# A branch prefetch hint on the tensor engine for the block that holds the general path

## The chip, the cores and the metric

The kernel runs on one core of a Trainium2 chip. The metric is device time in microseconds (us) of one execution, the median of three runs. Besides these runs there is one execution that the hardware profiler took; all rows below come from it. The engines are TensorE (PE: matrix products, with the weight load PEld beside it), VectorE (DVE), ScalarE (ACT), GpSimd (POOL) and SyncE (SP, which issues most transfers). Each engine runs its own stream of instructions; a q behind an engine's name means its sequencer, which reads that stream, branches, loads registers and waits on semaphores.

## The reference: three layers over 1536 tokens

```python
# linear attention with decay, 2 x 8 heads, 768 steps, head width 64
state = gamma * state + k_t v_t^T ;  y_t = scale * q_t state
# mixture of experts: 8 experts, 512 -> 1024 -> 512, one expert for a token
expert = argmax(x @ w_gate);  gate_w = softmax(x @ w_gate)[expert]
# an expert takes its first `capacity` (384) tokens, later ones give zeros
out = gate_w * (relu(x @ w1[expert]) @ w2[expert])
# feed-forward 512 -> 2048 -> 512 over all tokens
h = x @ w_in;  return (h * sigmoid(h)) @ w_out
```

## The kernel before

One function writes the whole program, in program order for each engine (a manual schedule). There are three stages.

The attention stage takes twelve blocks of 128 tokens. For each block it makes the scores, the head outputs and the state, then the gate: the expert of each token, its place among that expert's tokens (`place`) and one-hot rows from which the table of tokens for each expert is built. At its end `cnt` holds the number of tokens of each expert and `peak` the largest of them. The rows of expert 0 are transposed and split in two parts, `xthi` and `xtlo`, by `split_x` (line 555): ACT writes the high part in two casts, one for each 128 tokens, DVE the low part. The token table `tab_ps` of the other experts is made by twelve small matmuls (line 602).

Then comes the branch. An expert has `capm` = 216 slots here. The register `over` is loaded from `peak` on all five engines (line 670), and under `tc.If(over > capm)` (line 674) stands the general path: a loop over the experts that computes the tokens beyond 216. For the inputs that are timed no expert has more than 216 tokens, so each engine jumps over that block. On PE the general path is some 600 instructions of the compiled program.

Then follows the expert stage. For each of 8 experts `stage_a` (line 845, four times 24 matmuls, lines 854, 855 and 858, the product with w1) and `stage_b` (line 867, four times 24, lines 841 to 843, the product with w2). The weights come in 64 units of 512 KB: SP loads a unit into one of five `raw` buffers (line 140), ACT casts its high part `hi` (line 164) and DVE subtracts for the low part `lo` (line 168; POOL does it for units 0 and 1). Expert e uses units 8e to 8e+7 in order; `advance` (line 821) has ACT cast three units ahead of the one that PE takes up, ahead of that stage's own results on ACT and DVE. The feed-forward stage at the end is built in the same manner, and its rows leave by an indirect transfer.

The lines that the change and the steps below touch:

```python
528        if i == NT - 1:
529            run(fill)
530            fill = first_rows()
...
670    over = nc.values_load(
671        peak[0:1, 0:1], min_val=0, max_val=NTOK,
...
674    with tc.If(over > capm):
```

Of the kernel before, what the change touches and what calls it, by code (L numbers as in the profile page):

```python
# [92 lines left out]
def moe_chain_kernel(ctx: ExitStack, tc: tile.TileContext, cap: int, a, out: bass.AP):  # L93
# [4 lines left out]
    capm = min(cap, SL)  # L98
# [173 lines left out]
    def load_q(i):  # L272
        qs[i] = att.tile([P, DM], F32, tag="q", name=f"q{i}", bufs=3)
        kts[i] = att.tile([P, DM], F32, tag="kt", name=f"kt{i}", bufs=3)
        (nc.scalar if i == 0 else nc.sync).dma_start(out=kts[i], in_=a["kt"][i])
        nc.sync.dma_start(out=qs[i], in_=a["q"][i])

    def load_vk(i, parts=((0, 2),)):
        if i not in vks:
            vks[i] = att.tile([P, 2, DM], F32, tag="vk", name=f"vk{i}", bufs=3)  # L280
        src = a["vk"][i].rearrange("p (c x) -> p c x", c=2)
        for lo, hi in parts:
            nc.sync.dma_start(out=vks[i][:, lo:hi], in_=src[:, lo:hi])

    def load_gq(i):
        for h in range(2):
            nc.sync.dma_start(
                out=gq[h * 64 : (h + 1) * 64, :, i * P : (i + 1) * P],
                in_=gq_src[h, :, i * P : (i + 1) * P].partition_broadcast(64),
            )  # L290
# [34 lines left out]
    def scores(i):  # L325
        q, vk = qs[i], vks[i]
        c = i % TPB
        kt = kts[i]

        ap = [aps.tile([P, NP, P], F32, tag="A", name=f"A{i}_{g}", bufs=2) for g in range(2)]  # L330
        am = att.tile([P, 2, NP, P], F32, tag="am", name=f"am{i}")
        for pr in range(NP):
            for g in range(2):
                rows, cols = slice(g * 64, (g + 1) * 64), slice(pr * P, (pr + 1) * P)
                nc.tensor.matmul(ap[g][:, pr], lhsT=kt[rows, cols], rhs=q[rows, cols], start=True, stop=True)
        for g in range(2):
            nc.vector.tensor_tensor(out=am[:, g], in0=ap[g], in1=dec[:, g], op=ALU.mult)
        am_t[i] = am
        if c > 0:
            qg = att.tile([P, NP, P], F32, tag="qg", name=f"qg{i}")  # L340
            nc.gpsimd.tensor_tensor(
                out=qg, in0=q.rearrange("p (r t) -> p r t", r=NP),
                in1=gq[:, :, c * P : (c + 1) * P], op=ALU.mult,
            )
            qg_t[i] = qg
        if c < TPB - 1:
            vp = att.tile([P, H, D], F32, tag="vp", name=f"vp{i}")
            kq = cst[:, C_KQ + c * H : C_KQ + (c + 1) * H]
            nc.gpsimd.tensor_tensor(
                out=vp, in0=vk[:, 0].rearrange("p (h e) -> p h e", h=H),  # L350
                in1=kq.unsqueeze(2).to_broadcast([P, H, D]), op=ALU.mult,
            )
            vp_t[i] = vp

    def heads_out(i):
        b, c = divmod(i, TPB)
        vk = vks[i]
        yp = aps.tile([P, NP, P], F32, tag="y", name=f"y{i}")
        if c > 0:
            qg = qg_t.pop(i)  # L360
            for pr in range(NP):
                nc.tensor.matmul(
                    yp[:, pr], lhsT=sbd[:, pr].rearrange("p h e -> p (h e)"), rhs=qg[:, pr],
                    start=pr == 0, stop=False, skip_group_check=True,
                )
        am = am_t.pop(i)
        for h in range(H):
            nc.tensor.matmul(
                yp[h % 2 * 64 : (h % 2 + 1) * 64, h // 2], lhsT=vk[:, 0, h * D : (h + 1) * D], rhs=am[:, h % 2, h // 2],
                start=c == 0 and h < 2, stop=True, skip_group_check=True,  # L370
            )
        xt = att.tile([P, NP, P], F32, tag="xt", name=f"xt{i}")
        nc.scalar.copy(out=xt, in_=yp)
        xt_t[i] = xt
# [19 lines left out]
    def gate(i, fill):  # L394

        xt = xt_t.pop(i)
        gp = aps.tile([P, 2, 512], F32, tag="g", name=f"g{i}", bufs=2)
        sm = few.tile([P, 48], F32, tag="sm", name=f"sm{i}", bufs=3)
        for pr in range(NP):
            o = pr % 2 * GW  # L400
            nc.tensor.matmul(gp[:, pr // 2, o : o + GW], lhsT=xt[:, pr], rhs=eyewg[:, pr, :GW], start=True, stop=True)
        gv = gp[:, :, : 2 * GW].rearrange("p b (r x) -> p b r x", r=2)
        lg = sm[:, 8:16]
        nc.vector.tensor_reduce(
            out=lg, in_=gv[:, :, :, P:].rearrange("p b r e -> p e b r"), op=ALU.add, axis=mybir.AxisListType.XY
        )
        next(fill, None)
        m8 = sm[:, 0:8]
        nc.vector.max(out=m8, in_=lg)
        next(fill, None)  # L410
        nm = sm[:, 20:21]
        nc.vector.tensor_scalar(out=nm, in0=m8[:, 0:1], scalar1=-1.0, scalar2=None, op0=ALU.mult)
        i8 = few.tile([P, 8], U32, tag="i8", name=f"i8_{i}")
        nc.vector.max_index(out=i8, in_max=m8, in_values=lg)
        nc.scalar.activation(sm[:, 24:32], lg, AF.Exp, bias=nm, scale=1.0, accum_out=sm[:, 21:22])
        next(fill, None)
        ef = ecol[:, i : i + 1]
        nc.vector.tensor_copy(out=ef, in_=i8[:, 0:1])
        next(fill, None)
        oh = few.tile([P, 2 * E], BF16, tag="oh", name=f"oh{i}")  # L420
        nc.vector.tensor_scalar(out=oh, in0=iota_e2, scalar1=ef, scalar2=None, op0=ALU.is_equal)
        nc.vector.tensor_scalar(out=sm[:, 22:23], in0=sm[:, 21:22], scalar1=1e-9, scalar2=None, op0=ALU.add)
        nc.vector.reciprocal(out=sm[:, 23:24], in_=sm[:, 22:23])
        nc.gpsimd.tensor_tensor(out=soh[(i + 1) % 2], in0=soh[i % 2], in1=oh, op=ALU.add)
        rt[i] = (sm, gp, gv, oh)

    def store_x(i):
        sm, gp, gv, oh = rt[i]
        rows = slice(i * P + 1, (i + 1) * P + 1)
        xr = att.tile([P, DM], F32, tag="xr", name=f"xr{i}", bufs=3)  # L430
        nc.scalar.activation(
            xr.rearrange("p (b r x) -> p b r x", b=2, r=2), gv[:, :, :, :P], AF.Copy, scale=sm[:, 23:24]
        )
        nc.sync.dma_start(out=xtok[rows, :], in_=xr)
        xrs[i] = xr
# [64 lines left out]
    def first_rows():  # L500

        tp = aps.tile([P, 512], F32, tag="s", name="tab0")
        n = NT - NPATCH
        for i in range(n):
            nc.tensor.matmul(tp[:, :nmain], lhsT=ohps[:, i], rhs=ohbs[:, i, :nmain], start=i == 0, stop=i == n - 1)
        yield
        tok0 = few.tile([P, nmain], I32, tag="tok0", name="tok0", bufs=1)
        nc.vector.tensor_copy(out=tok0, in_=tp[:, :nmain])
        x0.extend(gather_rows(att, 0, j, "x0_", tok0, n) for j in range(nmain))

    def run(steps):
        for _ in steps:
            pass
# [5 lines left out]
    for i in range(NT):  # L519
        if i + 3 < NT:  # L520
            load_q(i + 3)
        if i + 2 < TPB:
            load_gq(i + 2)
        if i + 2 < NT:
            load_vk(i + 2)
        if i + 1 < NT:
            scores(i + 1)
        if i == NT - 1:
            run(fill)
            fill = first_rows()  # L530
        if i > 0:
            gate(i - 1, fill)
            run(fill)
            if i >= NT - 2:
                store_x(i - 1)
        heads_out(i)
        state(i)
        if i > 0:
            count(i - 1)
            fill = place(i - 1)  # L540
            if i >= NT - 2:
                for _ in range(2):
                    next(fill)
            else:
                store_x(i - 1)
        if i >= NT - 5:
            moe_feed.load_to(LOADS[i - NT + 5])
            if NT - 4 <= i < NT - 1:
                moe_feed.step()
# [113 lines left out]
    def place_reg(ap, lo, hi):  # L663
# [6 lines left out]
    over = nc.values_load(  # L670
        peak[0:1, 0:1], min_val=0, max_val=NTOK,
        skip_runtime_bounds_check_because="an expert's count lies between 0 and the number of tokens",
    )
    with tc.If(over > capm):  # L674
        with tc.tile_pool(name="gen", side="right", bufs=1) as gen, tc.tile_pool(name="gps", side="right", bufs=2, space=PSUM) as gps:
            places = Places(gen, "gen", True)
            places.tokens()
# [430 lines left out]
```

## Time and profile before

| | us |
|---|---|
| median of three runs | 530.82 |
| lowest and highest of them | 528.69, 532.09 |
| the profiled execution | 535.48 |
| its span, from the first instruction to the last | 533.7 |
| PE busy in that span | 513.0 |
| transfers of program code on queue q8 | 29 packets, 0.48 MB |

Times inside the profiled execution count from the start of the span. 1.78 us of its time lie outside the span. The granted clock of TensorE has two levels here: 1.00 is 2.4 GHz, 0.50 is 1.2 GHz.

### The profile page before, as it was taken

What the parts mean: (1) busy time and instruction counts of PE and PEld (TensorE: products, weight loads), DVE (VectorE), ACT (ScalarE), POOL (GpSimd) and SP (SyncE); (2) the same over time, 40 slices, a digit from 0 to 9 for tenths busy, and PEclk for the clock granted to TensorE, in tenths of its full rate; (3) what the DMA queues carried; (4) which work ended last, traced back from release to release, by engine and by line L of the source; (5) the groups of instructions that cost most, each with busy time, mean ns of one, the idle gap of its engine ahead of it and who ended that gap; (6) DMA issues with size and microseconds to landing.
All of it is one profiled execution on the core that took longest, in us unless ns stands there. A gap on an engine that the chain in (4) does not pass through costs nothing.

```text
span 533.7 us, 9254 instructions
## 1 busy us (share of the span) xinstructions
PE 513.0 (96%) x3590; PEld 460.9 (86%) x3590; DVE 326.7 (61%) x663; ACT 243.7 (46%) x404; POOL 152.5 (29%) x144
## 2 busy tenths in 40 slices
PE   7899797999999999999999999999999999999995
PEld 5898687999999999999988888888888888888884
DVE  2587843778898787786366675465566565332441
ACT  2345522555656656565255655553344542312110
POOL 2536521110543204421003352333232421000324
PEclk9899967999999999999999999999999999999998
DMA  8999932597776767765012231222111200000202
GB/s 271 293 328 312 337 120 82 167 348 234 244 253 226 268 214 262 258 217 198 0 41 79 80 118 41 79 80 67 52 54 65 80 0 1 0 1 0 80 38 119
DMA packets 27152, 76.12 MB, mean 143 GB/s; under 512 B 3553, under 2 KB 6497, under 8 KB 27106
## 3 DMA queue, kind: packets, MB, share of 16 engines
q1 hardware_dynamic: 24416, 67.53, 37.7%
q0 software_dynamic: 2256, 7.34, 3.9%
q8 instruction: 29, 0.48, 0.4%
q10 hardware_dynamic: 434, 0.64, 0.3%
q14 instruction: 17, 0.14, 0.1%
HBM read 69.20 MB, written 6.29 MB: 141 GB/s over the span
## 4 chain that ended last, share of the span: by engine, by line
PE 66%; issue 14%; POOL 2%; DVE 1%; POOLq 0%; ACT 0%; DVEq 0%; ACTq 0%
PE s L842 11%; PE s L841 11%; PE s L843 11%; PE h L855 6%; PE h L854 6%; PE h L858 6%; PE y L841 5%; PE y L843 5%; PE y L842 5%; POOL out L979 1%; PE xp L815 1%; POOL lo L203 0%; POOLq L1104 0%; POOL w L199 0%; DVE gv L950 0%
## 5 line engine op out<-in xcount | busy, mean ns | idle before, releaser
L199 POOL TENSOR_TENSOR w<-w,ex 128x512 f32<-128x512 f32 x32 | 41.4, 1292 | 223.9 <-DVE ex L196 223.9
L950 DVE TENSOR_TENSOR gv<-s,gv 128x512 f32<-128x512 f32 x48 | 33.2, 691 | 86.9 <-ACT gv L949 86.8
L168 DVE TENSOR_TENSOR lo<-raw,hi 128x1024 fp32r<-128x1024 f32 x62 | 82.0, 1337 | 3.2 <-issue 2.3
L841 PE MATMUL s<-x2hi,hi 128*128 128x512 f32 x192 | 74.7, 389 | 0.0
L843 PE MATMUL s<-x2hi,lo 128*128 128x512 f32 x192 | 74.7, 389 | 0.0
L842 PE MATMUL s<-x2lo,hi 128*128 128x512 f32 x192 | 74.7, 389 | 0.0
L949 ACT ACTIVATE gv<-s 128x512 f32<-128x512 f32 x48 | 28.7, 597 | 97.9 <-PE s L843 97.9
L841 PE MATMUL y<-hhi,hi 128*128 128x216 f32 x256 | 70.8, 277 | 0.0
L843 PE MATMUL y<-hhi,lo 128*128 128x216 f32 x256 | 70.3, 274 | 0.0
L842 PE MATMUL y<-hlo,hi 128*128 128x216 f32 x256 | 70.3, 274 | 0.0
L841 PE MATMUL s<-hi,ghi 128*128 128x512 f32 x176 | 68.5, 389 | 0.0
L842 PE MATMUL s<-lo,ghi 128*128 128x512 f32 x176 | 68.5, 389 | 0.0
L843 PE MATMUL s<-hi,glo 128*128 128x512 f32 x176 | 68.5, 389 | 0.0
L164 ACT CAST hi<-raw 128x1024 fp32r<-128x1024 f32 x64 | 65.6, 1048 | 2.7 <-issue 2.2
L854 PE MATMUL h<-xthi,hi 128*128 128x216 f32 x256 | 60.6, 279 | 3.5 <-PEq L674 3.5
L855 PE MATMUL h<-xthi,lo 128*128 128x216 f32 x256 | 60.5, 280 | 0.0
L952 DVE TENSOR_TENSOR glo<-gv,ghi 128x512 fp32r<-128x512 f32 x48 | 36.2, 755 | 33.0 <-ACT ghi L951 33.0
L203 POOL TENSOR_TENSOR lo<-w,hi 128x512 fp32r<-128x512 f32 x32 | 47.4, 1480 | 22.4 <-ACT hi L202 22.4
L854 PEld LDWEIGHTS h<-xthi,hi 128*128 128x128 f32 x256 | 50.5, 197 | 3.6 <-issue 3.6
L855 PEld LDWEIGHTS h<-xthi,lo 128*128 128x128 f32 x256 | 50.5, 197 | 0.0
L843 PEld LDWEIGHTS y<-hhi,lo 128*128 128x128 f32 x256 | 49.2, 192 | 0.0
L842 PEld LDWEIGHTS y<-hlo,hi 128*128 128x128 f32 x256 | 49.1, 192 | 0.0
(140 smaller groups left out, 948.6 us busy)
## 6 DMA issues: line engine op xcount, KB each, us to landing
raw<-w SPq DMA_DIRECT2D x64, 512.0 KB, 4.4
raw<-w_in SPq DMA_DIRECT2D x16, 512.0 KB, 3.3
raw<-w_out SPq DMA_DIRECT2D x16, 512.0 KB, 3.3
vk<-vk SPq DMA_DIRECT2D x11, 512.0 KB, 6.0
q<-q SPq DMA_DIRECT2D x12, 256.0 KB, 5.3
xtok<-xr SPq DMA_DIRECT2D x12, 256.0 KB, 4.9
kt<-kt SPq DMA_DIRECT2D x11, 256.0 KB, 6.3
gq<-gq SPq DMA_DIRECT2D x10, 128.0 KB, 4.7
```

Of the source, the lines that this page charges most:

```text
L164: nc.scalar.copy(out=hi, in_=t)
L168: lo_eng.tensor_tensor(out=lo, in0=t, in1=hi.bitcast(F32), op=ALU.subtract)
L199: nc.gpsimd.tensor_tensor(out=w, in0=w, in1=ex.bitcast(F32), op=ALU.mult)
L203: nc.gpsimd.tensor_tensor(out=lo[:, sl], in0=w, in1=hi[:, sl].bitcast(F32), op=ALU.subtract)
L841: nc.tensor.matmul(out_ap, lhsT=lh, rhs=rh, start=first, stop=False, skip_group_check=True)
L842: nc.tensor.matmul(out_ap, lhsT=lh, rhs=rl, start=False, stop=False, skip_group_check=True)
L843: nc.tensor.matmul(out_ap, lhsT=ll, rhs=rh, start=False, stop=last, skip_group_check=True)
L854: nc.tensor.matmul(hb[:, f], lhsT=whi[:, d, f], rhs=xhi[:, d], start=f == 0 and d == 0, stop=False, **skip)
L855: nc.tensor.matmul(hb[:, f], lhsT=wlo[:, d, f], rhs=xhi[:, d], start=False, stop=False, **skip)
L858: nc.tensor.matmul(hb[:, f], lhsT=whi[:, d, f], rhs=xlo[:, d], start=False, stop=d == KD - 1, **skip)
L950: nc.vector.tensor_tensor(out=gv, in0=hb, in1=gv, op=ALU.mult)
L952: nc.vector.tensor_tensor(out=glo, in0=gv, in1=ghi.bitcast(F32), op=ALU.subtract)
```

## The change

The `If` gets a label, and a hint for the branch of that label is marked for PE alone. It says that this branch is likely to be taken. `LikelyTaken` names the branch and not the block: the general path stands right behind the branch in PE's program, and the branch is taken when that path is skipped.

```diff
         if i == NT - 1:
+
+            tc.mark_branch_hint_location("over", "LikelyTaken", (mybir.EngineType.PE,))
             run(fill)
             fill = first_rows()
...
-    with tc.If(over > capm):
+    with tc.If(over > capm, label="over"):
```

The line stands in the last pass of the attention loop, but the built program has the hint at the start of PE's stream. This is the piece of the difference on PE at its first instructions (`warm` are products of zeros that PE starts with):

```order
-L1104 UNCONDITIONAL_BRANCH
+L1106 UNCONDITIONAL_BRANCH
+L1106 BRANCH_PREFETCH_HINT
 L266 LDWEIGHTS warm
 L266 MATMUL warm_99<-warm 128x512
```

One instruction is new, ahead of all matmuls; no other instruction of PE, and none of another engine, is added or moved. This is the place of the branch on PE, before, from the end of the attention stage into the general path (`gohp`, `gtp` are that path's tiles):

```order
L602 LDWEIGHTS ohps
L602 MATMUL tab_ps<-ohbs,ohps 128x16
L670 TENSOR_LOAD peak
L674 COMPARE_AND_BRANCH
L749 LDWEIGHTS gohp
L749 MATMUL gtp<-gohb,gohp 128x16
```

It reads the same after the change, two lines further down in the file. This is where the skipped block ends on PE, before, and the first matmul of the expert stage follows:

```order
L789 MATMUL gy_1446<-gh_1445,gw_7_1533 128x128 x8
L756 REGISTER_ALU
L756 COMPARE_AND_BRANCH
L756 UNCONDITIONAL_BRANCH
L674 UNCONDITIONAL_BRANCH x2
L854 MATMUL h_0_1575<-xthi_1161,hi_836 128x216
```

Here too nothing has moved. The general path's own loop holds a hint of the same kind in the program of before, and that loop isn't entered.

## Rows read from the trace of the kernel before

**Rows 1.** The page: busy time of each engine; granted clock in 40 slices, tenths.

```profile
PE 513.0 (96%) x3590; PEld 460.9 (86%) x3590; DVE 326.7 (61%) x663; ACT 243.7 (46%) x404; POOL 152.5 (29%) x144
PEclk9899967999999999999999999999999999999998
```

**Rows 2.** Waits of PE: total us, times, longest us.

```profile
PE h L854 <- PEq L674: 3.5, 1, 3.5
```

**Rows 3.** Windows: PE, PEld, DVE, ACT, POOL busy (instructions), clock, DMA share, GB/s.

```profile
81.20:84.70 3.50, 0.01 (x1) 0.01 (x1) 2.01 (x4) 1.26 (x2) 2.07 (x2) 0.86 0.18 42
84.70:90.50 5.80, 5.78 (x27) 5.80 (x28) 0.00 (x0) 0.32 (x1) 0.33 (x1) 0.50 0.47 162
95.60:530.00 434.40, 431.42 (x2698) 386.71 (x2696) 270.02 (x400) 207.38 (x323) 116.44 (x89) 1.00 0.35 120
```

**Rows 4.** Line 674 by engine: duration min/median/max in ns, first and last start us.

```profile
L674 SPq COMPARE_BRANCH  x1: 50/50/50, 78.8 to 78.8; - x1
...
L674 PEldq COMPARE_BRANCH  x1: 3847/3847/3847, 80.7 to 80.7; - x1
L674 ACTq COMPARE_BRANCH  x1: 45/45/45, 81.5 to 81.5; - x1
L674 DVEq COMPARE_BRANCH  x1: 72/72/72, 82.1 to 82.1; - x1
```

**Rows 5.** The page, queues that load program code: packets, MB, share of 16 engines' span.

```profile
q8 instruction: 29, 0.48, 0.4%
...
q14 instruction: 17, 0.14, 0.1%
```

**Rows 6.** The DMA view of 0 to 64.1 us, the same columns.

```profile
q8 instruction: 6, 0.10, 0.6%
```

**Rows 7.** The DMA view of 81 to 84.7 us.

```profile
q8 instruction: 1, 0.02, 1.6%
```

**Rows 8.** Timeline of PE at the start: start us, us, instruction, [idle before, releaser].

```profile
1.22 1.03 PE L266 MATMUL warm<-warm 128*128 128x512 bf16 x2 [1.22 <-DVE warm L260]
```

**Rows 9.** Timeline around the branch (columns as in the group before).

```profile
80.76 0.45 PE L602 MATMUL tab_ps<-ohbs,ohps 128*128 128x16 f16 x12
80.96 0.45 ACT L562 CAST xthi<-x0t 128x352 fp32r<-128x352 f32 x1 [0.31 <-PE x0t L570]
81.85 1.04 ACT L164 CAST hi<-raw 128x1024 fp32r<-128x1024 f32 x1 [0.44 <-ACTq L674]
...
82.93 1.23 DVE L168 TENSOR_TENSOR lo<-raw,hi 128x1024 fp32r<-128x1024 f32 x1 [0.88 <-DVEq L674]
...
84.18 0.34 SPq L140 DMA_DIRECT2D raw<-w  x1
...
84.72 0.52 PE L854 MATMUL h<-xthi,hi 128*128 128x216 f32 x1 [3.50 <-PEq L674]
```

**Rows 10.** Windows of PE alone: busy (instructions), clock, DMA share, GB/s.

```profile
84.72:89.94 5.22, 5.22 (x24) 0.50 0.52 180
89.94:92.91 2.97, 2.97 (x25) 0.90 0.00 0
...
95.59:98.27 2.68, 2.68 (x26) 1.00 0.00 0
```

**Rows 11.** An idle stretch of PE in the attention stage, by its timeline.

```profile
15.04 1.75 PE L362 MATMUL y<-qg,sbd 128*128 128x128 f32 x8 [1.66 <-POOL qg L341]
```

**Rows 12.** Windows behind that stretch (columns as in the third group).

```profile
15.40:18.90 3.50, 3.50 (x34) 3.27 (x34) 0.00 (x0) 0.16 (x1) 1.14 (x2) 0.51 1.05 304
```

**Rows 13.** Timelines of DVE, PE and ACT in the first expert.

```profile
96.45 1.22 DVE L168 TENSOR_TENSOR lo<-raw,hi 128x1024 fp32r<-128x1024 f32 x1
...
98.27 0.27 PE L841 MATMUL y<-hhi,hi 128*128 128x216 f32 x1
...
101.23 2.00 ACT L164 CAST hi<-raw 128x1024 fp32r<-128x1024 f32 x2 [2.23 <-issue]
```

**Rows 14.** DMA issues of the weight units: KB, median us to landing.

```profile
raw<-w SPq DMA_DIRECT2D x64, 512.0 KB, 4.4
```

## The prediction

> **What bounds the kernel now.** I read the page first. PE is busy 513.0 of 533.7 us [rows 1], so what the change can give is what PE loses between its matmuls, and the list of PE's waits is the view for that. Its longest entry is the one that the change aims at: 3.5 us ahead of the first expert matmul, at line 854, released by PE's own sequencer at line 674, the branch [rows 2]. No engine and no transfer is named there: PE waits for itself. The windows then tell whether the time lost there comes back. Behind it, from 95.6 to 530 us, PE is busy 431.42 of 434.40 us at full clock, and the missing 2.98 us are the end, where the last rows leave [rows 3]. So from the branch on PE sets the pace, and a stretch taken out ahead of it ends up in the time. The same windows show a second loss: in 84.7 to 90.5 us, right behind the gap, the granted clock is 0.50, the lower of the two levels [rows 3].
>
> Line 674 by engine says what the branch costs. SP, ACT and DVE take it in 50, 45 and 72 ns; PE takes 3847 ns over the same comparison with the same outcome [rows 4]. What differs on PE is the length of the code that is jumped over, and that code was being loaded: the trace has two queues that load program code, and q8 must be mostly PE's, since it carries 0.48 of the 0.62 MB [rows 5] while PE issues 7180 of the 8391 working instructions [rows 1]. q8 moved six blocks in the first 64.1 us [rows 6], and then one inside the very gap, between 81 and 84.7 us [rows 7]. I read this as: PE reaches the branch, has the code behind it and not the code at its target, and stands until that block has come. That this is the cause is inference; the rows give place and time, not the reason.
>
> **The change part by part.**
>
> *The new instruction itself.* It is one sequencer instruction at the head of PE's stream, where PE waits 1.22 us for the zeros that DVE writes [rows 8]. It costs nothing while that wait covers it. Without the cover its nearest rows are the branches of 45 to 72 ns [rows 4], 0.07 us at most. If it loads one block more, that is 1 of 29 on q8, which takes 0.4% of the DMA time as a whole [rows 5]: nothing.
>
> *The gap.* If the target's code is there, PE's branch should cost what it costs the others, and the gap is set by what is late next. PE's last matmuls end at 80.76 + 0.45 = 81.21 us. The first matmul at line 854 reads both halves of `xthi`, and ACT ends the second at 80.96 + 0.45 = 81.41 [rows 9]. Three rows bound what then is left of the 3.50 us. The least is PE starting right at that cast: 84.72 − 81.41 = 3.31 us gained. ACT's own passage over the same branch left 0.44 us idle, DVE's 0.88 [rows 9]; with these on PE the gain is 3.50 − 0.44 = 3.06 or 3.50 − 0.88 = 2.62 us. I take 3.06, since ACT's branch is the plain case of 45 ns, and keep 2.62 to 3.31. Next late after it: `xtlo` is read only 16 matmuls later, and DVE was done with it before it waited 0.88 us ahead of 82.93, so by 82.05 [rows 9]; 16 matmuls at the full rate (2.68 us for a stage of 24) take 1.79 us from 81.65, so it is not late.
>
> *The clock.* PE's first stage behind the gap took 5.22 us for 24 matmuls at 0.50; the same stage at full clock takes 2.68 [rows 10]. The next one ran partly slow, 2.97 us. If PE no longer stands still there, I expect the clock to stay at the level it had before the gap, and the gain is (5.22 − 2.68) + (2.97 − 2.68) = 2.83 us. For this speaks that it fell elsewhere too behind a shorter stop: PE idle 1.66 us up to 15.04, then 0.51 in the window from 15.4 to 18.9 [rows 11, 12]; 0.44 us is well below either. The ends are 0 (it falls all the same, or did not fall in the executions that are timed) and 2.90 (half of the 5.80 us window at 0.50).
>
> *Does it last?* Two things could take it back. First, `lo` of unit 4: DVE ends it at 96.45 + 1.22 = 97.67 and PE takes that unit up at 98.27 [rows 13], only 0.60 us later. But that subtraction stands behind results of `stage_a` on DVE, and those follow PE, so it moves along. Second, the transfers that don't follow PE: unit 7 is issued at 84.18, once DVE has `lo` of unit 2 [rows 9]; by the median of 4.4 us [rows 14] it lands near 88.6, and ACT casts it at 101.23 [rows 13], or 95.3 when all is 5.9 us earlier. Still 6.7 us of room. So I take nothing off.
>
> *Sum.* 3.06 + 2.83 = 5.89 us. The profiled execution would go from 535.48 to 529.59. It stands 4.66 us above the median of the runs shown, but the terms are waits and rates of PE that do not depend on that, so I take the same 5.89 from the median: 530.82 − 5.89 = **524.9 us**, 1.1% faster.
>
> **The rivals.**
>
> *The hint does nothing by the time it is needed.* It stands at the head of the stream and the branch comes 80.7 us later, with six blocks loaded on q8 between [rows 6]. If the block that it names is pushed out by those, or it is forgotten, the 3847 ns remain: 530.8 us. Nothing in the trace shows a hint at work; the only ones in the program of before are in a loop that isn't entered. For the forecast speaks that a hint placed that far ahead is only of use if it is kept until its branch; that is an argument about its purpose, not a row. The Trainium skill (Runtime: NRT & Kernel Launch, section on instruction fetch mechanics) is on this rival's side: it says that prefetch is purely sequential, and that a taken branch out of the loaded window forces a fetch before execution goes on. The trace agrees with the second half (a q8 block in the gap), and no run here shows whether a hint is an exception to the first. By that rule the time would be 530.8.
>
> *The gap closes, the clock is no better.* Then 530.82 − 3.06 = 527.8 us, 0.6% faster. For it: the three runs of before differ by 3.4 us, more than this whole term, so the clock may not fall at the same place in every execution. Against: in the profile it fell behind both stops of PE that I looked at.
>
> *The gain is given back in the feed.* If `lo` of unit 4 stays at 97.67, PE meets it 0.60 us earlier than now and no more: 530.2 us. Against it stands the order on DVE, above.
>
> *Slower.* The hint is carried out where it stands, and the block that it loads takes the place of the one that comes next in PE's stream. Then PE stops once early, for as long as at the branch, and the branch still stops it: 530.82 + 3.85 = 534.7 us, and with a second fall of the clock (2.83) 537.5. It decides when PE first leaves the code that it started with; PE is stopped by others for 1.66 us ahead of 15.04 anyway [rows 11], which would hide some of it. Nothing in the trace speaks for it, and nothing excludes it.
>
> **How the numbers follow.** Forecast (both terms) 0.55; gap alone 0.22; hint without effect 0.15; given back 0.03; slower 0.05. The two that make no difference and the slower one hold 0.23 between them, mostly for want of a row that shows a hint. A change of 1% is 5.3 us, and about what a measurement of this kernel can tell from no change. The forecast's own ends are 2.62 + 2.83 = 5.45 and 3.31 + 2.90 = 6.21 us of gain, 525.4 to 524.6, close to that line, and with medians that wander as the three runs do about a fifth of it falls on the near side: faster by over 1% 0.45. The slower case passes 1% (536.1) only with the clock's fall as well: 0.03. Within 1%: 0.52. Range: 523.0 below, the forecast's low end with 1.6 us for the spread of the runs; 530.8 above, which takes in the gap alone and half of the cases without effect. That leaves out the slower case, the other half, and a little below: some 0.18.
>
> **What would show it.** In the profile after: PE's branch at line 674 well under 0.1 us instead of 3847 ns; the wait of line 854 on PE's sequencer gone, its first matmul between 81.4 and 82.1 us; one block of q8 more ahead of 80.7 us; granted clock 1.00 from there through the second stage; a first stage of 2.68 us; a span near 527.8. If the branch is short and the stage still takes 5.22 us, the clock's term was wrong; if the branch is still 3.8 us, the hint is lost on the way; a new stop of PE in the first 20 us is the slower case. What would make it wrong beyond these is a wait behind the branch that the 3.50 us now cover, and which I haven't seen.

## The result and the profile after

The kernel with the hint takes 523.33 us (median of 6 runs, 521.98 to 525.57) beside 531.46 for the one before (6 runs, 528.29 to 535.47). The ratio is 0.987 with an interval of 0.983 to 0.991; of 531.46 us that is 6.7 us less, between 4.7 and 8.8. The forecast was 5.9 less: 524.9 us, in a range from 523.0 to 530.8. The medians themselves lie 8.1 apart.

The span of the profiled execution fell from 533.7 to 520.2 us, by 13.5, more than the times did. Three windows sort this out. They are cut at the end of the last `tab_ps` product (81.21 us before, 80.76 + 0.45 in [rows 9]) and at the start of the last matmul. Windows of PE alone in the profile after (stretch, its length, PE busy with its instructions, granted clock, DMA share, GB/s):

```profile
0.00:74.93 74.93, 66.55 (x822) 0.98 0.89 296
74.93:514.45 439.52, 439.26 (x2768) 1.00 0.36 122
514.45:520.20 5.75, 0.28 (x3) 0.70 0.21 87
```

And the same cut before:

```profile
0.00:81.21 81.21, 70.72 (x822) 0.92 0.83 273
81.21:526.74 445.53, 442.03 (x2769) 0.99 0.35 120
526.74:533.70 6.96, 0.28 (x3) 0.80 0.18 71
```

From the table to the last matmul the time went from 445.53 to 439.52: 6.01 us, where the sum was 5.89. The rest of the 13.5 is 6.28 us of the attention stage and 1.21 from the start of the last matmul on, and I don't put it down to the hint. Over all profiles the table ends anywhere from 74.93 to 82.39 us: from 74.93 to 80.42 with the hint on PE, from 75.16 (where only the other engines have it) to 82.39 without. Part of it I put down to the clock. In the profile before it stood at 0.50 from 66.7 to 76.9 us, in the one after at 1.00 there; a kernel with the hint below has the same fall, from 65.0 to 75.2 us, and the first profile of the short kernel without a hint has none there.

The waits of PE, in us in total, times, longest; the sequencer is no longer among them:

```profile
PE A L335 <- DMA q<-q: 3.9, 2, 2.2
...
PE h L856 <- ACT xthi L564: 0.3, 1, 0.3
```

The branch by engine (duration min/median/max in ns, start in us; two lines further down than in [rows 4]):

```profile
L676 SPq COMPARE_BRANCH  x1: 50/50/50, 72.7 to 72.7; - x1
L676 PEldq COMPARE_BRANCH  x1: 392/392/392, 74.4 to 74.4; - x1
L676 ACTq COMPARE_BRANCH  x1: 45/45/45, 75.2 to 75.2; - x1
L676 DVEq COMPARE_BRANCH  x1: 72/72/72, 75.8 to 75.8; - x1
```

The timeline around it, as in [rows 9]:

```profile
74.48 0.45 PE L604 MATMUL tab_ps<-ohbs,ohps 128*128 128x16 f16 x12
74.68 0.45 ACT L564 CAST xthi<-x0t 128x352 fp32r<-128x352 f32 x1 [0.31 <-PE x0t L572]
75.19 0.37 PE L856 MATMUL h<-xthi,hi 128*128 128x216 f32 x1 [0.26 <-ACT xthi L564]
```

The branch runs from 74.4 to 74.8 us, beside the last `tab_ps` products, and the next work of PE waits for ACT's cast, which ends at 74.68 + 0.45 = 75.13; 0.06 us later PE starts. So 0.26 us of the 3.50 in [rows 9] are left. And the two stages behind it, PE alone, which answer to [rows 10]:

```profile
75.19:77.96 2.77, 2.77 (x24) 1.00 0.17 25
77.96:80.64 2.68, 2.68 (x26) 1.00 0.72 216
```

The granted clock is 1.00 through both. The page counts the blocks of program code, beside the 29 of [rows 5]:

```profile
q8 instruction: 28, 0.46, 0.3%
```

### The profile page after: what moved, and what is told of

It is laid out like the page before. It is cut to its first block, busy times and chain, and to the rows that moved or that the text cites. A ratio compares the mean times of both kernels' runs of the same rounds, so it can differ in the third digit from the quotient of the medians.

```text
span 520.2 us, 9255 instructions
## 1 busy us (share of the span) xinstructions
PE 506.1 (97%) x3590; PEld 454.1 (87%) x3590; DVE 319.9 (61%) x663; ACT 243.7 (47%) x404; POOL 152.6 (29%) x144
## 4 chain that ended last, share of the span: by engine, by line
PE 74%; issue 14%; DMA 5%; POOL 3%; DVE 2%; ACT 0%; POOLq 0%; SPq 0%; DVEq 0%; ACTq 0%
PE s L843 11%; PE s L844 11%; PE s L845 11%; PE h L856 6%; PE h L857 6%; PE y L843 6%; PE y L845 5%; PE y L844 5%; PE h L860 5%; DMA q<-q 4%; PE A L335 2%; POOL out L981 2%; PE y L368 1%; PE g L401 1%; DMA gq<-gq 1%
## 5 line engine op out<-in xcount | busy, mean ns | idle before, releaser
L856 PE MATMUL h<-xthi,hi 128*128 128x216 f32 x256 | 58.9, 274 | 0.3 <-ACT xthi L564 0.3
L857 PE MATMUL h<-xthi,lo 128*128 128x216 f32 x256 | 58.8, 274 | 0.0
L856 PEld LDWEIGHTS h<-xthi,hi 128*128 128x128 f32 x256 | 49.1, 192 | 0.4 <-ACT xthi L564 0.4
L857 PEld LDWEIGHTS h<-xthi,lo 128*128 128x128 f32 x256 | 49.1, 192 | 0.0
```

The costliest lines, as they stand in the source:

```text
L856: nc.tensor.matmul(hb[:, f], lhsT=whi[:, d, f], rhs=xhi[:, d], start=f == 0 and d == 0, stop=False, **skip)
L857: nc.tensor.matmul(hb[:, f], lhsT=wlo[:, d, f], rhs=xhi[:, d], start=False, stop=False, **skip)
```

## The experiments

The theory is that of the prediction: PE stands because the code at the branch's target isn't loaded, the hint has it loaded, and the clock then stays up. Rival A: PE's branch is slow for another reason, such as waiting until the queued matmuls are done. Rival B: the gap alone counts, and the clock costs nothing outside this one profile. Rival C: it isn't the load but the new instruction as such, or what it does to the attention stage. The last runs ask how the hint uses the loader. Each ratio is to the kernel before, timed on the same chip in turn.

**The skipped block made short.** The kernel before without the loop over the experts in the general path, so that the branch jumps over less. That loop, which isn't entered, is left out with the three lines behind it.

```diff
     with tc.If(over > capm):
...
-        with tc.For_i(0, E, 1) as e:
...
```

> No hint. The general path leaves out its loop over the experts (not entered with these inputs), so on PE some 30 instructions stand behind the branch instead of some 600. Theory (PE stands because the code at the branch's target is not loaded): the branch on PE takes 0.05 to 0.4 us instead of 3.85, PE's gap ahead of line 854 is 0.2 to 0.9 us instead of 3.50, the first stage takes 2.7 us, and the time is that of the hinted kernel: ratio to before 0.984 to 0.991. Rival A (a branch on PE is slow whatever it jumps over, because its sequencer first has to see the queued matmuls done): the branch stays at 3.8 us, the ratio is 0.998 to 1.002.

526.36 us (10 runs), ratio 0.992 [0.989, 0.995], just above what was expected; in a second set 523.35 (6 runs), 0.989 [0.986, 0.992]. Without any hint PE's branch (line 674, then the waits) does what it does after the change:

```profile
L674 PEldq COMPARE_BRANCH  x1: 228/228/228, 77.7 to 77.7; - x1
```

```profile
PE h L808 <- ACT xthi L562: 0.3, 1, 0.3
```

From the table to the last matmul both profiles take 439.52 us, the same as with the hint; the window of the first:

```profile
78.21:517.73 439.52, 439.26 (x2768) 1.00 0.36 122
```

So the stop goes with the length of the block that is jumped over, and the stop with the clock is worth what the hint gave.

**The stop covered.** 14 products of zeros behind the last `tab_ps` product, so that PE has work queued while its sequencer stands at the branch.

```diff
+    keep_warm(14, "warm_over")
     split_x(0, tv0)
```

> No hint, and 14 more matmuls of zeros with 512 columns on PE after the token table, ahead of the branch; they keep PE busy for about 14 x 0.22 = 3.1 us while the branch waits. Theory (the gap costs twice, once by itself and once by the clock behind it): the branch stays at 3.8 us and the first expert matmul comes as late as before, but PE is idle for under 1 us, the clock stays at 1.00, the first stage takes 2.7 instead of 5.2 us; the time falls by 2.7 us, ratio 0.995. Rival B (the clock falls there in the profiled execution alone, or for another reason): ratio 1.000. Rival A (the branch waits for the queued matmuls): the zeros come on top, the first expert matmul 3.1 us later, ratio 1.001 to 1.006.

530.13 us (12 runs), 1.001 [0.998, 1.004]. PE's branch, then the zeros (the trace has 13 of the 14):

```profile
L675 PEldq COMPARE_BRANCH  x1: 3521/3521/3521, 78.3 to 78.3; - x1
```

```profile
78.02 2.97 PE L266 MATMUL warm_over<-warm 128*128 128x512 bf16 x13
```

The branch starts with the zeros still to run and is no longer than without them (3847 ns before), and it ends 0.85 us behind them, where it ended 3.34 us behind the last product before. If it waited for the queued matmuls first, the zeros would come on top: Rival A falls, as it does by the 228 ns of the short block. Two windows, PE, PEld, DVE, ACT and POOL busy, clock, DMA share, GB/s, show the idle stretch and the first stage:

```profile
80.99:82.16 1.17, 0.00 (x1) 0.03 (x1) 0.00 (x0) 0.00 (x0) 0.78 (x1) 1.00 0.65 196
82.16:84.90 2.74, 2.74 (x24) 2.74 (x25) 0.00 (x0) 0.00 (x0) 0.00 (x0) 1.00 0.88 277
```

Behind an idle stretch of 1.17 us the clock stayed at 1.00. In the profile the table to the last matmul took 443.45 us, 2.08 less than before and not 2.7, because the zeros themselves put off the branch: the first expert matmul came 4.21 us behind the table instead of 3.51. The times don't show even the 2.08 (the interval goes from 1.2 us less to 2.0 more). Taken alone this is for Rival B, and it stays open why.

**The branch turned round.** The same hint, with the block placed so that the hinted branch leads into the general path and isn't taken; the jump past that path is a branch of its own, without a hint.

```diff
-    with tc.If(over > capm, label="over"):
+    with tc.If(over > capm, label="over", preferred_fallthrough_block=False):
```

> The same hint instruction at the same place, but the program is laid out so that the hinted branch leads into the general path and isn't taken; the jump over that path is then an unconditional one, without a hint. Theory: the jump still costs 3.5 us of PE idle, with the slow first stage behind it: ratio 0.997 to 1.003. Rival C (the gain comes from the new instruction as such, for instance by shifting the code or its loading, and with it the attention stage, which ended 6.3 us earlier in the profile with the hint): ratio 0.984 to 0.991, the attention stage as short as in the hinted kernel.

531.93 us (12 runs), 1.001 [0.998, 1.005]. The first of PE's two branches takes 104 ns, and the jump 3298:

```profile
L676 PEldq COMPARE_BRANCH  x2: 104/1701/3298, 76.8 to 77.6; - x2
```

```profile
PE h L856 <- issue: 3.6, 1, 3.6
```

```profile
80.91:85.31 4.40, 4.40 (x25) 0.61 0.60 208
```

The instruction of the hint is there, at the same place, and gives nothing when it names the other side: Rival C falls. The clock cost less here, 4.40 − 2.68 = 1.72 us in the first stage: it was at 1.00 until 81.7 us and then for a shorter time at 0.50.

```profile
80.91:81.70 0.79, 0.79 (x7) 1.00 0.64 182
81.70:85.10 3.40, 3.40 (x19) 0.50 0.62 225
```

**Before and after once more.**

> The kernel before, unchanged, for a second profile and its scatter. Theory: PE's gap is 3.4 to 3.6 us again; the end of the attention stage (the last matmul of the token table), 81.2 us in the first profile, moves by several us from one execution to the next, so that its 6.3 us are not the hint's; ratio 0.997 to 1.003. Rival C: it ends at 81 us again, within 1 us.

532.38 us (12 runs), 1.002 [0.998, 1.005], the branch at 3607 ns, the stop, and the clock behind it (PE's wait, then the first stage alone):

```profile
PE h L854 <- PEq L674: 3.3, 1, 3.3
```

```profile
85.66:90.88 5.22, 5.22 (x24) 0.50 0.56 186
```

> The hinted kernel, unchanged, for a second profile and more runs. Theory (only the gap and the clock behind it): ratio 0.985 to 0.992 in runs, as for the short path without a hint (0.9919); in the profile the span from the last matmul of the token table to the last matmul of all is 439.5 us again, against 445.5 and 445.3 in the two profiles of before; the end of the attention stage is anywhere in 74 to 83 us. Rival C (the hint speeds up the attention stage too): it ends at 75 us again, ratio 0.985 or less.

524.37 us (6 runs), 0.987 [0.982, 0.992]; the branch at 392 ns again, 0.25 us of gap, and 439.52 us from the table to the last matmul. Stop and clock belong to the one kernel and not to one execution of it, and the attention stage, which ended at 78.16 us here, doesn't come out short each time.

**The hint on all engines, and on all but PE.**

```diff
-            tc.mark_branch_hint_location("over", "LikelyTaken", (mybir.EngineType.PE,))
+            tc.mark_branch_hint_location("over", "LikelyTaken", tuple(mybir.ALL_ENGINES))
...
+            tc.mark_branch_hint_location("over", "LikelyTaken", tuple(e for e in mybir.ALL_ENGINES if e != mybir.EngineType.PE))
```

> The hint on all five engines instead of PE alone. Theory (PE sets the pace behind the branch, so the idle 0.88 us of DVE and the 1.3 us of SP at their branches cost nothing): DVE's and SP's idle at the branch shorter by some 0.5 to 1 us, PE's first expert matmul unchanged, ratio to before within 0.004 of the hint on PE alone. Rival (DVE's or SP's branch still holds up PE): a further 0.5 to 1 us, 0.001 to 0.002, hardly to be told apart in time, but PE's gap of 0.26 us would shrink.

526.01 us (12 runs), 0.992 [0.989, 0.995]: not better than PE alone, and perhaps a little worse, though the intervals meet. That the other engines would stand less was not borne out. The other engines' branches became longer, and DVE's idle time there didn't change:

```profile
L676 SPq COMPARE_BRANCH  x1: 70/70/70, 74.0 to 74.0; - x1
L676 PEldq COMPARE_BRANCH  x1: 392/392/392, 75.7 to 75.7; - x1
L676 ACTq COMPARE_BRANCH  x1: 68/68/68, 76.5 to 76.5; - x1
L676 DVEq COMPARE_BRANCH  x1: 84/84/84, 77.1 to 77.1; - x1
```

```profile
DVE lo L168 <- DVEq L676: 0.9, 1, 0.9
```

> The hint on ACT, DVE, POOL and SP, not on PE. Theory: PE's branch takes 3.3 to 3.9 us, its gap is 3.3 to 3.6 us, the last us are 6.9: ratio 0.997 to 1.003. Rival (the idle 0.88 us of DVE or the 1.3 us of SP at their branches hold up the weights): ratio 0.996 or less, DVE's idle under 0.5 us.

529.67 us (12 runs), 1.000 [0.996, 1.004]. The stop is back, and the slow stage behind it:

```profile
PE h L856 <- PEq L676: 3.2, 1, 3.2
```

```profile
78.36:83.58 5.22, 5.22 (x24) 5.22 (x25) 0.00 (x0) 0.00 (x0) 0.63 (x1) 0.50 0.57 189
```

The table ended at 75.16 us here, so a short attention stage isn't what the hint on PE brings. In these two profiles, and not in those of the kernels before and after, ACT stands 2.0 and 2.5 us in the first expert ahead of a cast of `hi`, and PE waits a little later for a `lo`. The rows are of the hint on all engines and of the hint on all but PE:

```profile
ACT hi L164 <- DVE lo L168: 2.0, 1, 2.0
PE y L845 <- DVE lo L168: 0.2, 1, 0.2
...
ACT hi L164 <- DVE lo L168: 2.5, 1, 2.5
PE y L845 <- DVE lo L168: 0.9, 1, 0.9
```

From the table to the last matmul they took 439.98 us beside 439.52, and 446.23 beside 445.53. A block of q14 is loaded during each of ACT's two stops, so I take them for late code, as in the last experiment below; no run shows that cause.

**What the clock costs, seven times over.** The kernel after, with a stop of PE ahead of each of the experts 1 to 7: a small product on PE that waits for ACT and four operations of GpSimd. Once nothing fills the stop, once 14 products of zeros do.

```diff
+    def stop(e, yb):
+        nc.scalar.copy(out=big, in_=yb[1][:, 0])
+        for _ in range(4):
+            nc.gpsimd.tensor_tensor(out=big, in0=big, in1=big, op=ALU.mult)
+        wp = bank(f"stop{e}")
+        for _ in range(14):   # none in the idle version
+            nc.tensor.matmul(wp, lhsT=zeros[:, :P], rhs=zeros, start=True, stop=True)
+        nc.tensor.matmul(wp[:, :P], lhsT=big[:, :P], rhs=ident, start=True, stop=True)
     for e in range(E):
+        if e > 0:
+            stop(e, yb)
```

> The hinted kernel with seven more stops of PE, one ahead of each of experts 1 to 7: a small matmul waits for a chain of one copy on ACT and four products on POOL, begun when the expert before is done, about 3 us. Theory (a stop of PE of some 3 us costs itself and then the clock, 1.7 to 2.9 us as in the profiles): 7 x (3 + 2.3) = 37 us over the hinted kernel, about 561 us, the clock at 0.50 behind the stops in the profile. Rival B (the clock's fall costs nothing outside the profile, or falls rarely): 7 x 3 = 21 us, about 545 us.

585.83 us (6 runs), 1.102 [1.097, 1.108], beside 561 and 545 expected: the waits were longer than planned, 37.4 us in place of 21, which isn't the whole difference. PE's wait at the stops, and two of the stages behind them:

```profile
PE stop L1012 <- POOL big L1008: 37.4, 7, 6.7
```

```profile
107.30:112.60 5.30, 5.30 (x25) 0.50 0.86 325
...
199.50:204.70 5.20, 5.20 (x25) 0.50 0.64 224
```

> The same seven waits, but 14 matmuls of zeros with 512 columns stand ahead of each, so PE works while it waits. Theory: the delay of 3.1 to 3.5 us each stays, the clock does not fall: 7 x 3.3 = 23 us over the hinted kernel, about 547 us, and 12 to 20 us below the kernel with the idle stops. Rival B: the same time as with the idle stops, within 3 us.

576.28 us (6 runs), 1.085 [1.080, 1.090]. Here the clock stays up at five of the stops, whose idle rest behind the zeros is 1.62 to 2.35 us, and it falls at the two where that is 3.65 us; the rows are a kept one and a fallen one:

```profile
108.00:113.00 5.00, 5.00 (x45) 1.00 0.91 350
137.40:143.40 6.00, 6.00 (x28) 0.50 0.30 87
```

The difference is 9.55 us in the times and 10.0 between the two spans (586.5 and 576.5), for five falls: 1.9 us each. The expected 12 to 20 was too high, since two falls were left and the stops were longer than planned. But it is in the times of unprofiled runs, so a fall of the clock costs time there too. Rival B falls for these stops; for the one at the branch the covered stop stays on its side.

**The hint where the target is near anyway.** The short block (again without the general path's loop) with the hint on PE.

> The short path (the general path leaves out its loop over the experts, not entered with these inputs) together with the hint on PE. There is no far code for the hint to fetch. Theory (the hint saves the load of the target and nothing else): the same as the short path alone, ratio 0.988 to 0.995, PE's gap 0.26 us, and from the start of the last matmul to the end 6.6 us as there. Theory with a second effect (in the five profiles with a hint that led the right way those last us were 5.5 to 6.0 instead of 6.6 to 6.9): they are under 6.1 us here too, and the time is 1 us, 0.002, below the short path alone.

527.58 us (12 runs), 0.997 [0.995, 1.000]. Neither time that was expected came: the same program without the hint gave 523.35 on the same chip, so the hint cost about 4 us. The branch is short (262 ns) and the gap 0.25, but PE stops a little later, between its fourteenth matmul and the next:

```profile
80.44 0.28 PE L811 MATMUL h<-xthi,lo 128*128 128x216 f32 x1
82.51 0.37 PE L810 MATMUL h<-xthi,hi 128*128 128x216 f32 x1 [1.79 <-issue]
```

The code shows why. Without the hint one block of q8 comes between 60 and 78.5 us; with it none does between 60 and 79.5, and one comes at the stop, from 79.87 to 81.12 us (windows of the DMA view, first 60 to 78.5 without the hint, then 79.5 to 82.5 with it):

```profile
q8 instruction: 1, 0.02, 0.3%
```

```profile
q8 instruction: 1, 0.02, 2.6%
```

Both have 28 blocks in all. So the hint adds no load to those that PE makes anyway; as I read it, it puts off the next block in order. Here the target needed no load of its own, and that next block, which PE did need, came late: PE goes on 1.39 us after it has landed. The clock fell to 0.50 behind that stop, at 84.1 us.

## Why the prediction was right

**What bounds it.** PE's time between matmuls became the kernel's time, as the reading of [rows 1 to 3] had it: 6.01 us between table and last matmul, 6.7 by the ratio.

**The cause.** What was marked as inference is now shown as far as runs can: a shorter way to the target removes the stop without a hint, a hint to the other side doesn't, and hints on the other engines don't. The reading of q8 in [rows 7] was right, and holds in each of the five profiles with a long branch: one block of q8 is loaded during it, and it ends 1.37 to 1.52 us after that block has landed (before: landed at 83.16, branch over at 84.55). During none of the short ones does q8 load anything.

**The new instruction.** It takes 0.05 us at 0.84, inside PE's wait of [rows 8], and costs nothing, as forecast.

**The gap.** 3.50 to 0.26 us is 3.24, forecast 3.06 between 2.62 and 3.31. The choice of ACT's 0.44 us as the remainder was the small error. PE started 0.06 us behind the cast, near the end of the bound that let it start right there. "Well under 0.1 us" for the branch was wrong: it took 392 ns, but beside the last `tab_ps` products and ahead of ACT's cast, so that none of it shows.

**The clock.** 5.22 + 2.97 became 2.77 + 2.68: 2.74 us, forecast 2.83. The 0.09 is the first stage, whose first matmul takes 0.37 us instead of 0.28. How long the clock stays down behind a stop of this length differs: with the branch turned round the first stage lost only 1.72 us to it. And that this term counts in the times at the branch itself rests on the sum: 3.24 us of gap alone is under the 4.7 that the interval begins with, and under the 4.5 of the second set.

**Does it last.** Nothing was given back: 439.52 us in both profiles of the kernel after, in both of the short block, and 1.00 for the clock over that stretch.

**The chances, and luck.** The terms add up to 5.98 us of the 6.01. That the time came out more than 1% lower had 0.45, less than the 0.52 for a difference within 1%; the median of 523.33 lies only 0.3 us above the low end of the range, and the span of 520.2, far under the 527.8 that was named, owes most of that to the attention stage.

**One block more on q8** was wrong, and is the step that failed, though it had no price in the sum. There are six blocks ahead of the branch in both kernels, and 28 in all instead of 29. As I read it, the target's block is among the six, in the place of the one behind the branch, which only the general path would have used, and the load in the gap fell away. The same wrong picture of a load made in addition stood behind the expectation for the short block with the hint, and there it had a price.

**The rivals.** The hint held though it stands 74 us ahead of its branch. The Trainium skill (Runtime: NRT & Kernel Launch, section on instruction fetch mechanics) says that prefetch is purely sequential; the branch at 392 ns instead of 3847 speaks against that where a hint is set. The rival that ended slower had its mechanism half right, if my reading of the blocks holds: one does take another's place. But not where the hint stands: q8 moves nothing in the first 10 us of either kernel, and PE has no new stop there. It happens near the branch, and it did harm where the block put off was needed first, 1.79 us and a fall of the clock in the short kernel.

## What to carry to other kernels

Here a branch taken over a long block stopped PE for 3.2 to 3.6 us while the code at its target was loaded, and since PE set the pace, that was paid in full, and once more in the clock behind it. Look for a wait on an engine's own sequencer at a branch, and compare the same branch on the other engines. The hint on PE alone took away all but 0.26 us of the stop. On the four other engines, whose branches took 45 to 72 ns, it gained nothing, and with it ACT stood 2.0 and 2.5 us in the first expert. In the short kernel, where the branch was short without a hint, the hint cost about 4 us. So measure a hint engine by engine, and check the count of code blocks ahead of the branch and the first stages behind it.

## What the runs showed that was not expected

The hint is, by all the rows show, remembered rather than carried out at once. It stands at the head of PE's stream, q8 moves nothing for 10 us, and the sixth block ahead of the branch comes between 60 and 70 us in the kernels before and after alike. With the branch turned round, and with the short block and the hint, that sixth block is missing. My reading, not shown, is that the loader takes the hinted block when it would load the one behind the branch.

PE's branch takes 392 ns with the hint, 262 with hint and short block, 228 with the short block alone and 104 where it falls through, against 45 to 72 on the other engines; the hint itself made those 68 to 84. The reason for either is open.

Attention stage and end vary for one and the same program: the short kernel's table ended at 78.21 and 77.19 us in its two profiles, and from the start of the last matmul to the end it took 6.64 and 5.46. The end goes with the chip that ran: 6.64 to 6.92 us in the four profiles of one chip, 5.45 to 5.96 in the seven of another, with the hint and without. Which chips the first two profiles come from isn't known, but nothing here makes their 1.21 us, or the 6.28 of the attention stage, a part of the gain.
